# Longer runs for one weight matrix, and two array columns in place of four for another, in a decode step bound by its loads

## The chip, the cores and the metric

One core of a Trainium2 chip runs the program. The metric is device time in microseconds (us). A profile of one execution goes with each kernel; its span counts from the first to the last instruction and is some 2.3 us shorter than the time of the same execution. In its lines PE is the matmul engine (TensorE) and PEld its weight loads, DVE is VectorE, ACT ScalarE, POOL GpSimd, and SPq is the queue from which SyncE issues the loads. What is said of single DMA packets is read from the packet records in the traces, which none of the views shown here prints. One execution of the kernel before took 426.16 us. It is slow in the sense used here (over 1.5% above the fastest).

## The reference, cut to what matters

```python
x = A_x                                   # [1, 1, 1024]
xn = layernorm(x)
# A: one query token, 32 heads in 4 groups of 8, 65536 cached keys per group, head size 128
q = xn @ wq                               # [1024, 4096]
p = softmax(q k^T / sqrt(128)); o = p v   # 4 x 8 heads
A = o.reshape(1, 1, 4096) @ wo            # wo: [4096, 1024]
# B: a small MLP on the same row
x1 = xn + shifted(gelu(layernorm(xn) @ w1)) @ w2
B = x1 + gelu(layernorm(x1) @ w3) @ w4    # w3: [1024, 3584], w4: [3584, 1024]
out = x + A + B
```

With a sequence of one token the shifts leave only zeros. What is large is what has to be read: eight loads of 8.4 MB of keys, eight of values, and 35.7 MB of weights.

## The kernel before

Everything large passes through three slots of 64 KB per partition in one fixed order. A load is issued when the slot that it takes is free.

```python
stream = ["wq", "w3", "w12"]
for u in range(NU):                       # NU = 8
    if u == NU - 1:
        stream += [("K", u), "wo", ("V", u)]
    else:
        stream += [("K", u), ("V", u)]
stream.append("w4")
# ... (cut) in the loader: wo as 4 runs of 16 KB per partition, one per group
elif it == "wo":
    go(out=t[:].rearrange("p (g n) -> p g n", g=HKV),
       in_=A_wo.rearrange("(g p j) n -> p g (j n)", g=HKV, p=P))
```

The input row of w3 is replicated over a strip of 32 columns of the array (called one array column below), and four such array columns work side by side. Each reads every 28th column of w3, so that the hidden vector comes out in the order in which w4 is laid out.

```python
def row_matmul(acc, rep, cols, widths, groups=4):
    for c in range(DC):
        for i, n in enumerate(widths):
            for q in range(groups):
                nc.tensor.matmul(acc[32 * q:32 * q + 32, i, 0:n], lhsT=rep[:, c, :], rhs=cols(c, i, q),
                                 start=(c == 0), stop=(c == DC - 1),
                                 tile_position=(0, 32 * q), skip_group_check=True)

def compute_w3():
    wt = st.tiles["w3"][:, 0:DC * F].rearrange("p (c m k) -> p c k m", c=DC, k=FC)   # FC = 28
    psh = ps_S.tile([P, SUBS, 512], F32, name="psh", tag="sc")
    row_matmul(psh, xn2_rep, lambda c, i, a: wt[:, c, 16 * i:min(16 * (i + 1), FC), 32 * a:32 * (a + 1)],
               (512, 32 * FC - 512))
    st.done("w3")                         # frees the slot: V0 may be issued
    # ... (cut) two GELUs, a transpose, two copies into hT
```

The projection of the first three groups takes 48 matmuls with `oT[g][:, j]` (8 heads' worth of one group, laid out as wo's rows ask for) while V7 is still arriving; the last group's 16 come at the end.

## Time and profile before

| | kernel before |
|---|---|
| time | 400.77 us, median of 3 (400.53 to 426.16) |
| span of the profiled execution | 398.4 us |
| bytes loaded | 169.87 MB |
| time of the DMA packets, share of 16 engines' span | 99.0% |
| busiest engine | PE, 59% |

When the second and third slot were refilled for the first time, from the timeline of the DMA queue's issuer (start, length, what):

```profile
51.34 0.33 SPq L225 DMA_DIRECT2D big<-in_A_v_cache_dram  x1
58.04 0.33 SPq L225 DMA_DIRECT2D big<-in_A_k_cache_dram  x1
```

and what w3's matmuls cost, from the page's groups (operation, count, busy us, mean ns, idle before):

```profile
L330 PE MATMUL psh<-big,ln_rep_b 128*32 128x512 bf16 (+1 forms) x64 | 12.5, 947 | 3.0 <-DMA big<-in_B_w_dram 3.0
```

V0 is issued the moment the last of these is done (38.81 + 12.49 = 51.30 us).

### The profile page before, as it was taken

To read this page: it belongs to the slowest core of one execution; us is meant where nothing else is said; L and a number is where in the kernel's file an instruction comes from. 1 tells how busy PE (TensorE), PEld (TensorE's weight loads), DVE (VectorE), ACT (ScalarE), POOL (GpSimd) and SP (SyncE) were. 2 spreads that over 40 slices of the span, in tenths; PEclk is the share of its full clock that TensorE was granted. 3 is DMA by queue.
4 is the path that set the end of the run, shared out by engine and by line. 5 is a ranking of instruction groups with operands and counts; after the bars stand their busy time and mean duration, and the time that the engine had idled before them with its cause. 6 is when DMAs were issued, how large, how long until landed. Compare 5 with 4: busy or idle time off the path is not lost.

```text
span 398.4 us, 2623 instructions
## 1 busy us (share of the span) xinstructions
PE 234.3 (59%) x1372; PEld 45.1 (11%) x862; DVE 211.4 (53%) x162; ACT 27.9 (7%) x36; POOL 10.1 (3%) x38
## 2 busy tenths in 40 slices
PE   0283970591469238833974196529652956394986
PEld 0200010010100010011001010100020102000133
DVE  0602010974196569543963795259429942894132
ACT  1002010003000200020002000200010001002000
POOL 2200000000000000000000000000000000002000
PEclk9997996598869785956796889567955895698899
DMA  9998999999999999999999999999999998999996
GB/s 421 421 449 375 441 447 474 441 421 421 416 422 434 421 474 449 421 428 421 421 429 434 454 454 428 416 428 421 434 442 428 461 434 387 413 457 429 407 428 267
DMA packets 4310, 170.03 MB, mean 427 GB/s; under 512 B 457, under 2 KB 459, under 8 KB 844
## 3 DMA queue, kind: packets, MB, share of 16 engines
q1 hardware_dynamic: 4294, 169.87, 99.0%
q8 instruction: 9, 0.15, 0.1%
q14 instruction: 1, 0.01, 0.0%
q10 hardware_dynamic: 6, 0.00, 0.0%
HBM read 169.87 MB, written 0.00 MB: 426 GB/s over the span
## 4 chain that ended last, share of the span: by engine, by line
DMA 54%; DVE 21%; PE 18%; ACT 2%; another core or an unknown queue 2%; SPq 1%; POOLq 1%; issue 1%; DVEq 0%; ACTq 0%
DMA big<-in_A_k_cache_dram 41%; DVE big L410 15%; PE sc L415 11%; DMA big<-in_B_w_dram 8%; DMA big<-in_A_wq_dram 5%; PE oacc L465 4%; PE psq L330 2%; DVE p_sb L436 2%; DVE mx L420 2%; ACT p_sb L433 2%; SPq L217 1%; POOLq L613 1%; ACT L433 0%; DVE m L424 0%
## 5 line engine op out<-in xcount | busy, mean ns | idle before, releaser
L415 PE MATMUL sc<-big,qdiag 128*128 128x512 bf16 x512 | 130.7, 417 | 63.8 <-DVE big L410 63.8
L410 DVE STREAM_TRANSPOSE big<-big 128x4096 f32<-128x4096 f32 x32 | 139.4, 4412 | 47.9 <-DMA big<-in_A_k_cache_dram 47.8
L465 PE MATMUL oacc<-big,p_sb 128*32 128x512 bf16 x512 | 44.7, 518 | 34.5 <-DVE p_sb L436 34.5
L420 DVE TENSOR_REDUCE mx<-sc 128x1 f32<-128x2048 f32 x8 | 18.3, 2292 | 30.5 <-PE sc L415 30.5
L415 PEld LDWEIGHTS <-qdiag 128*128 128x128 bf16 x128 | 13.3, 104 | 176.6 <-issue 146.1
L433 ACT ACTIVATE p_sb<-sc,nball 128x2048 bf16<-128x2048 f32 x8 | 15.7, 1967 | 218.5 <-DVE nball L431 218.5
L436 DVE STREAM_TRANSPOSE p_sb<-p_sb 128x2048 bf16<-128x2048 bf16 x8 | 18.5, 2311 | 18.0 <-ACT p_sb L433 18.0
L465 PEld LDWEIGHTS <-p_sb 128*32 128x32 bf16 x512 | 16.5, 125 | 59.4 <-DVE p_sb L436 35.1
L474 DVE SCALAR_TENSOR_TENSOR og<-oacc,wb,og 128x512 f32<-128x512 f32 x4 | 3.0, 751 | 29.1 <-PE oacc L465 29.1
L508 PE MATMUL o_acc<-big,oT 128*1 128x512 bf16 x48 | 13.0, 440 | 2.4 <-ACT p_sb L433 2.4
L330 PE MATMUL psh<-big,ln_rep_b 128*32 128x512 bf16 (+1 forms) x64 | 12.5, 947 | 3.0 <-DMA big<-in_B_w_dram 3.0
L422 PE MATMUL pm_mx<-ident_f,mx 128*1 128x128 f32 x8 | 2.2, 270 | 19.1 <-DVE mx L420 19.1
L330 PE MATMUL psq<-big,ln_rep_a 128*32 128x512 bf16 x64 | 9.9, 486 | 3.9 <-DMA big<-in_A_wq_dram 3.9
L355 POOL COPY qdiag<-qx 32x32 bf16<-32x32 bf16 x16 | 3.3, 205 | 263.1 <-PE sc L415 245.4
L371 DVE STREAM_TRANSPOSE h_row<-h_row 128x896 bf16<-128x896 bf16 x1 | 1.1, 1111 | 16.2 <-ACT h_row L370 16.2
L343 DVE CAST q_row<-psq 64x1024 bf16<-64x1024 f32 x1 | 1.2, 1217 | 12.7 <-PE psq L330 12.7
L273 PE MATMUL pm_ln<-ln_rowsum_a,ones_f 128*128 128x1 f32 x2 | 0.6, 346 | 12.5 <-DVE ln_rowsum_a L271 12.5
L264 DVE STREAM_TRANSPOSE x_t<-x_row 32x256 bf16<-32x256 bf16 x4 | 2.5, 616 | 8.1 <-DMA x_row<-in_A_x_dram 8.0
L487 PE MATMUL pm_e<-ol,sel8big 128*128 128x129 f32 x6 | 1.8, 385 | 7.9 <-DVE ol L485 7.9
L259 PE MATMUL psB<-big,hT 128*32 128x512 bf16 x46 | 5.5, 380 | 0.8 <-DMA big<-in_B_w_dram 0.8
L429 PE MATMUL pm_mx<-ident_f,rep 1*128 1x1 f32 x8 | 1.8, 229 | 5.0 <-DVE rep L426 5.0
L471 ACT COPY og<-oacc 128x512 f32<-128x512 f32 x4 | 2.3, 586 | 33.9 <-PE oacc L465 25.4
(112 smaller groups left out, 77.3 us busy)
## 6 DMA issues: line engine op xcount, KB each, us to landing
big<-in_A_wo_dram SPq DMA_DIRECT2D x1, 8192.0 KB
big<-in_B_w_dram SPq DMA_DIRECT2D x1, 7168.0 KB
big<-in_B_w_dram SPq DMA_DIRECT2D x3, 2048.0 KB
big<-in_B_w_dram SPq DMA_DIRECT2D x1, 2816.0 KB
big<-in_B_w_dram SPq DMA_DIRECT2D x1, 1280.0 KB
big<-in_B_w_dram SPq DMA_DIRECT2D x1, 512.0 KB
big<-in_B_w_dram SPq DMA_DIRECT2D x1, 256.0 KB
big<-in_A_k_cache_dram SPq DMA_DIRECT2D x8
```

What stands on the lines that cost most here:

```text
L217: go(out=t[i0:i0 + 4 * k:4, WHOLE * D:(WHOLE + m) * D].rearrange("e (i n) -> e i n", i=m), in_=w4_v[m0:m0 + k * m, WHOLE, :].rearrange("(i ...
L259: return nc.tensor.matmul(psB[32 * j:32 * j + 32, :], lhsT=lhsT.to_broadcast([lhsT.shape[0], 32]), rhs=rhs, start=start, stop=False, tile_ ...
L330: nc.tensor.matmul(acc[32 * q:32 * q + 32, i, 0:n], lhsT=rep[:, c, :], rhs=cols(c, i, q), start=(c == 0), stop=(c == DC - 1), tile_positio ...
L355: nc.gpsimd.tensor_copy(out=qdiag[at, LEAD:].rearrange("p (x c) -> p x c", x=4)[:, :, 32 * a:32 * a + 8], in_=qx[at, :, 8 * g:8 * g + 8])
L410: nc.vector.transpose(out=words, in_=words)
L415: nc.tensor.matmul(sc[:, e, :], lhsT=qdiag[:, c0:c0 + P], rhs=cols[:, s, e, :, b2, :, r], start=(s == 0 and b2 == 0 and r == 0), stop=(s = ...
L420: nc.vector.reduce_max(out=mx[:], in_=sc[:].rearrange("p e n -> p (e n)"), axis=AX.X)
L433: nc.scalar.activation(out=p_sb[:], in_=sc[:], func=ACTF.Exp, bias=nball[:, b:b + 1], scale=SCALE, accum_out=group["lall"][:, b:b + 1])
L436: nc.vector.transpose(out=flat, in_=flat)
L465: mm = nc.tensor.matmul(oacc[32 * q:32 * (q + 1), :], lhsT=pT[:, e, 32 * t:32 * (t + 1)], rhs=vt[:, :, e, t, :], start=(e == 0 and t < 4), ...
L508: nc.tensor.matmul(tail["rows"][0:1, h2, :], lhsT=oT[g][:, j:j + 1], rhs=wt[:, g, j, 512 * h2:512 * (h2 + 1)], start=(g == 0 and j == 0), ...
L613: with _tile.TileContext(nc) as tc:
```

## The change

Its intent is to read wo with larger packets. The first 3072 rows, three groups of 1024, become one load in which each partition gets 24 neighbouring rows, 48 KB in one piece. Row 24p + i then lies on partition p, whereas the attention results of group g lie with row 1024g + 8p' + j on partition p'. Both agree when i = 8k + j and 3p + k = 128g + p'. So nine one-hot matmuls, one for each k and g, move the results to their new partitions. The last group is ready too late for that and keeps its layout, in a second load. Besides, w3 runs on two array columns in place of four, with four GELUs of 64 partitions in place of two of 128.

```diff
             elif it == "wo":
-                go(out=t[:].rearrange("p (g n) -> p g n", g=HKV),
-                   in_=A_wo.rearrange("(g p j) n -> p g (j n)", g=HKV, p=P))
+                go(out=t[:, 0:EARLY * D], in_=A_wo[0:EARLY * P, :].rearrange("(p i) n -> p (i n)", p=P))
+                go(out=t[:, EARLY * D:], in_=A_wo[EARLY * P:, :].rearrange("(p j) n -> p (j n)", p=P))
...
-        row_matmul(psh, xn2_rep, lambda c, i, a: wt[:, c, 16 * i:min(16 * (i + 1), FC), 32 * a:32 * (a + 1)],
-                   (512, 32 * FC - 512))
+        halves = (slice(0, 16), slice(16, FC))
+        row_matmul(psh, xn2_rep, lambda c, i, q: wt[:, c, halves[i % 2], 32 * (q + 2 * (i // 2)):32 * (q + 2 * (i // 2) + 1)],
+                   (512, 32 * FC - 512) * 2, groups=2)
...   (four GELUs in place of two: cut)
+    def regroup():
+        pick3 = ogpool.tile([P, P * (2 * HKV - 3)], BF16, name="pick3", tag="og")
+        nc.gpsimd.memset(pick3[:], 0.0)
+        nc.gpsimd.tensor_copy(out=pick3[:, P * (HKV - 2):P * (HKV - 1)], in_=ident_f[:])
+        pm = ps_M.tile([P, 512], F32, name="pm_o", tag="pm")
+        for k in range(HKV - 1):
+            for g in range(HKV - 1):
+                at = P * (HKV - 2) + k - P * g
+                nc.tensor.matmul(pm[:, 8 * k:8 * k + 8], lhsT=pick3[:, at:at + 3 * P - 2:3], rhs=oT[g][:],
+                                 start=(k == 0 and g == 0), stop=(g == HKV - 2), skip_group_check=True)
+        nc.vector.tensor_copy(out=o_early[:], in_=pm[:, 0:EARLY])
...   (project(g) split in project_early() and project_last(), same matmuls: cut)
     for u in range(NU - 1):
         compute_k(u)
+        if u == NU - 2:
+            regroup()
         compute_v(u)
```

More of the change, by code (lines that the diff above doesn't have):

```diff
@@ L155 @@
     LEAD = 8 * (SETS - 1)
+    EARLY = 8 * (HKV - 1)
     const = ctx.enter_context(tc.tile_pool(name="const", bufs=1))
@@ L316 @@
         nc.vector.tensor_copy(out=x_halves[32 * j:32 * j + 1, :], in_=x_row[0:1, 512 * j:512 * (j + 1)])
+    o_early = const.tile([P, EARLY], BF16, name="o_early")
     place = ogpool.tile([P, LEFT, P], BF16, name="place", tag="og")
@@ L364, in compute_w3 @@
         psh = ps_S.tile([P, SUBS, 512], F32, name="psh", tag="sc")
-        row_matmul(psh, xn2_rep, lambda c, i, a: wt[:, c, 16 * i:min(16 * (i + 1), FC), 32 * a:32 * (a + 1)],
-                   (512, 32 * FC - 512))
+        halves = (slice(0, 16), slice(16, FC))
+        row_matmul(psh, xn2_rep, lambda c, i, q: wt[:, c, halves[i % 2], 32 * (q + 2 * (i // 2)):32 * (q + 2 * (i // 2) + 1)],
+                   (512, 32 * FC - 512) * 2, groups=2)
         st.done("w3")
         h_row = ppool.tile([P, 32 * FC], BF16, name="h_row", tag="p")
-        nc.scalar.activation(out=h_row[:, 0:512], in_=psh[:, 0, :], func=ACTF.Gelu_apprx_tanh)
-        nc.scalar.activation(out=h_row[:, 512:], in_=psh[:, 1, 0:32 * FC - 512], func=ACTF.Gelu_apprx_tanh)
+        for i in range(4):
+            a, part = 64 * (i // 2), slice(512 * (i % 2), (512, 32 * FC)[i % 2])
+            nc.scalar.activation(out=h_row[a:a + 64, part], in_=psh[0:64, i, 0:part.stop - part.start],
+                                 func=ACTF.Gelu_apprx_tanh)
         nc.vector.transpose(out=h_row[:], in_=h_row[:])
@@ L499, in group_rows, with project_early, project_last @@
         nc.vector.tensor_scalar(out=oT[g][:], in0=o5[:], scalar1=rl[:, 0:1], scalar2=None, op0=ALU.mult)
-    def project(g):
-        wt = st.tiles["wo"][:].rearrange("p (g j n) -> p g j n", g=HKV, j=8)
+    def regroup():
[9 more added lines that the diff above has]
+        nc.vector.tensor_copy(out=o_early[:], in_=pm[:, 0:EARLY])
+    def project_early():
+        wt = st.tiles["wo"][:].rearrange("p (i n) -> p i n", n=D)
+        for i in range(EARLY):
+            for h2 in range(2):
+                nc.tensor.matmul(tail["rows"][0:1, h2, :], lhsT=o_early[:, i:i + 1], rhs=wt[:, i, 512 * h2:512 * (h2 + 1)],
+                                 start=(i == 0), stop=(i == EARLY - 1), tile_position=(0, 0))
+    def project_last():
+        wt = st.tiles["wo"][:].rearrange("p (i n) -> p i n", n=D)
         for j in range(8):
             for h2 in range(2):
-                if g == HKV - 1:
-                    mm = row_acc(h2, oT[g][:, j:j + 1], wt[:, g, j, 512 * h2:512 * (h2 + 1)])
-                    continue
-                nc.tensor.matmul(tail["rows"][0:1, h2, :], lhsT=oT[g][:, j:j + 1],
-                                 rhs=wt[:, g, j, 512 * h2:512 * (h2 + 1)], start=(g == 0 and j == 0),
-                                 stop=(g == HKV - 2 and j == 7), tile_position=(0, 0))
-        return mm.ins if g == HKV - 1 else None
+                mm = row_acc(h2, oT[HKV - 1][:, j:j + 1], wt[:, EARLY + j, 512 * h2:512 * (h2 + 1)])
+        return mm.ins
     def copy_projection():
@@ L536 @@
     tail["rows"] = ps_S.tile([P, SUBS, 512], F32, name="o_acc", tag="sc")
-    for g in range(HKV - 1):
-        project(g)
+    project_early()
     copy_projection()
@@ L551 @@
     with tc.issue_after(filled):
-        projected = project(HKV - 1)
+        projected = project_last()
     quarters = [ps_M.tile([P, 512], F32, name="pm_r", tag="pm") for _ in range(2)]
```

## The prediction

> **What bounds the kernel now.** I read, in this order: the strip of 40 slices, the table of DMA queues, the windows over single loads, what the DMA queue itself waits for, the chain at the end of the span, and last the records of the single DMA packets. From the page:
>
> ```profile
> span 398.4 us, 2623 instructions
> PE 234.3 (59%) x1372; PEld 45.1 (11%) x862; DVE 211.4 (53%) x162; ACT 27.9 (7%) x36; POOL 10.1 (3%) x38
> ...
> DMA  9998999999999999999999999999999998999996
> ...
> q1 hardware_dynamic: 4294, 169.87, 99.0%
> ```
>
> No engine is busy over 59%, but the 16 DMA engines are busy in 99.0% of the span, with no slice under 8 tenths before the last. So the kernel is a stream of 169.87 MB: wq, w3, w1 and w2, then seven K and V pairs, K7, wo, V7, w4. Its three SBUF slots are refilled early enough that the queue never runs dry. Every number of the chain of waits that reads DVE or PE is an engine waiting its turn inside that stream, not a limit. The windows below split the stream at the packets' starts: wo, V7, the two together, and a pair of plain cache loads (V6 and K7). Columns: stretch, length, busy times, clock, DMA share, GB/s.
>
> ```profile
> 337.45:357.54 20.09, 13.76 (x68) 1.76 (x25) 17.09 (x4) 0.59 (x1) 0.00 (x0) 0.81 0.99 421
> 357.54:376.38 18.84, 13.06 (x49) 2.10 (x21) 6.18 (x10) 2.24 (x3) 2.23 (x1) 0.82 1.02 443
> 337.45:376.38 38.93, 26.82 (x117) 3.86 (x46) 23.28 (x13) 2.83 (x4) 2.23 (x1) 0.81 1.01 431
> 298.75:337.45 38.70, 22.28 (x120) 4.26 (x76) 25.92 (x16) 2.06 (x2) 0.00 (x0) 0.75 1.00 434
> ```
>
> wo's own window and V7's trade time at their border (the engines are not in step, their completions lie 2 us apart), so only the pair is safe: 38.93 us with wo, 38.70 us for an equal 16.8 MB without. The short runs of wo cost **0.23 us** in all. That is the whole of what this part of the change can win.
>
> The issue side is early. In the queue's own timeline wo is issued at 324.12 and its first packet goes at 337.45:
>
> ```profile
> 324.12 0.39 SPq L205 DMA_DIRECT2D big<-in_A_wo_dram  x1
> 338.94 0.34 SPq L225 DMA_DIRECT2D big<-in_A_v_cache_dram  x1
> 363.92 2.45 SPq L217 DMA_DIRECT2D big<-in_B_w_dram  x3
> ```
>
> And the end of the span hangs on the last landing of w4 (chain of waits, last part): the last four matmuls, one addition and the store follow it within 2.0 us.
>
> ```profile
> 384.19 12.15 DMA big<-in_B_w_dram
> ...
> 396.38 0.34 PE pm_r L578 x2
> ```
>
> **What the Trainium skill says.** "DMA: Bandwidth & Descriptors", Where 436 GB/s comes from: the SBUF ports cap the traffic at 435 GB/s. The trace agrees, 434 GB/s over the pair of cache loads: nothing can be won on those. The same page, Why small descriptors are slow (HBM only), puts a fixed cost of about 3 cycles on each packet and calls grouping worth it only at 256 B or less. The trace agrees that the cost is fixed and small: packets of 16 KB took 612.5 ns in the median, of 56 KB 2116 ns, of 64 KB 2420 ns, with 4 ns between packets; per byte 16 KB is 1.2% dearer than 64 KB. "SBUF — State Buffer", Specifications, gives lines of 16 bytes and a penalty for each access that crosses to a new line. w3 is read with a step of 28 elements, 56 bytes, so each element is on a new line; its 512-column matmuls took 1052 ns, against 486 ns for wq's, which read runs of 64 bytes, so the trace fits, though wq's also differ in running on two array columns. "TensorE: Matmul & The Clock Gate", Measured speedup vs the span model, gives 2.38 times for three column tiles: four columns at once should beat two unless reading is the limit. No run here has w3 both ways.
>
> **The change part by part.**
>
> *wo in two loads.* Before, each DMA engine carries 8 partitions x 4 runs of 16 KB: 32 x (612.5 + 4) = 19.73 us. After, 8 runs of 48 KB and 8 of 16 KB. I interpolate a 48 KB packet between 16 and 56 KB: 2116 - 8192 x (1503.5 / 40960) = 1815 ns. So 8 x 1819 + 8 x 616.5 = 19.48 us: 0.25 us less, minus one more 9 ns completion. The other way: 24 packets per engine more than a cache load cost 0.23 us, and 16 of them go: 0.15 us. **Saved: 0.15 to 0.24 us**, all on the path that sets the end, because every later load moves up by it.
>
> *One more issue and one more completion counter.* 0.4 us on the queue's issuer, 13 us before the load starts: hidden. The built order shows the counters of w4's pieces shifted by one place; the waits among them remain on the same kind of load (V7 for the eighth piece, the 2 MB piece for the last), so the queue stays fed.
>
> *Nine one-hot matmuls.* They come after K6's scores and before V6, where PE waits 4.75 us for the transposed probabilities (327.6 to 332.3). 128x128 weight loads took 104 ns in the score loop; with strided one-hot weights I take up to 200 ns, and as much per tiny matmul: 9 x 0.2 to 0.4 = 2 to 3.5 us, inside the gap. The extra DVE copy of 24 columns (0.16 us, as for the similar 128x1 copy) stands in DVE's wait for K7; the memset and cast on POOL (under 1 us, from 2.23 us for w4's memset of eight times the bytes) are far earlier than needed. Even 1 us of slip would only move V7's issue from 338.94 to 340, needed by about 356: hidden.
>
> *Projection.* 48 matmuls on the first three groups before and after, 16 on the last; same shapes, same place: 0.
>
> *w3 on two columns.* 64 matmuls remain. Now they take 12.49 us (38.81 to 51.30). If reading limits all columns together, it stays near 12.5 us; if each column has its own limit, two columns take twice, 25 us. The four GELUs on 64 partitions cost 2 x (0.60 + 0.48) = 2.16 us in place of 1.08. Both delay only V0's issue (51.34) and K1's (58.04). V0's first packet is due at 66.5; a load's first packet comes 1.0 us after issue (first load), so there are 14 us of slack. 12.5 us of delay still fits, 1.5 us short of the edge. K1 has over 25 us. Time on the path: **0**.
>
> Sum: 400.77 - 0.2, about 400.5 us.
>
> **The rivals.**
>
> (a) *The whole saving is real but drowned.* The three runs of before hold two at 400.53 and 400.77: their difference equals the effect. This is what I expect.
>
> (b) *w3 doubles and starves the queue.* For: four strided columns deliver 3584 columns per 1.54 us, some 0.58 per ns and column, which looks like a limit of each column. Against: the 14 us of slack. If it overran, the gap would be 0 to 2 us once, in the slices near 66 us, and the time up to 402.5 us.
>
> (c) *Long runs change how the engines stagger.* Eight 16 KB instruction fetches inside the stream each delay one DMA engine by 1.0 to 1.5 us, on different engines, so completions of the late loads spread over 2.07 us against 0.51 us at first, and the slowest sets each landing. If the added instructions make two fetches hit one engine, the end moves by up to 1.5 us; for the better, likewise. It is not tied to the idea of the change.
>
> (d) *16 KB runs cost more in memory than their packets show.* Then wo's gain would be over 1 us. Against: the pair of windows holds the entire cost, 0.23 us.
>
> **Range and chances.** The centre is 400.5. (a) gives -0.25 to 0; (b) and (c) have perhaps one chance in six together of +0.5 to +2; runs of one kernel differ by 0.1 to 0.3%, up to 1.2 us either way. So 399.7 to 401.5. Two per cent is 8 us, more than any rival yields: 0.97 for within 2%, and the rest for slow executions (one of before's three took 426.16) or what I didn't see.
>
> **What will show it right or wrong.** The DMA share stays at 99%, with 256 packets fewer on the queue and 16 completions more, some 4054. wo with V7 takes 38.7 to 38.8 us in place of 38.93. V0 is issued between 51 and 65 us and the first loads' stretch has no gap. The nine matmuls lie in PE's gap before V6. The last landing is near 396.1 in place of 396.38. I am wrong if the time moves by over 1 us; if a zero shows in the strip near 66 us; if PE, not the DMA, ends the wait before the last matmuls; or if wo's stretch shrinks by over 0.5 us.

## The result, and the profile after

The changed kernel took **400.65 us** (median of 6, 400.43 to 400.88), the kernel before 400.78 us (median of 6). The ratio is 0.9998 with a 95% interval of 0.9984 to 1.0012. A ratio here is the mean time of one kernel's fast runs over the mean of the other's in the same rounds (a round runs each kernel of a group in turn), so it is not quite the ratio of the medians. The time alone cannot show an effect of 0.15 us, so the profile has to.

The page of the changed kernel (span; busy us, share and instructions of each engine; DMA share in 40 slices; the data queue's packets, MB and share):

```profile
span 398.3 us, 2631 instructions
## 1 busy us (share of the span) xinstructions
PE 247.7 (62%) x1381; PEld 46.0 (12%) x855; DVE 211.2 (53%) x163; ACT 28.9 (7%) x38; POOL 11.0 (3%) x40
...
DMA  9998999999999999999999999999999999999996
...
q1 hardware_dynamic: 4054, 169.87, 99.0%
```

There are 240 packets fewer on the queue (256 data packets fewer, 16 completions more), as worked out beforehand, and the share is unchanged at 99.0%. PE gained 13.4 us of busy time and the span did not notice.

The stretch of wo and V7, and the pair of plain cache loads ahead of it, in the changed kernel (stretch, length, busy times, clock, DMA share, GB/s). A stretch is cut where the last packet of a load starts: this one from K7's last packet to V7's.

```profile
337.43:376.22 38.79, 26.42 (x113) 3.71 (x42) 23.28 (x13) 2.83 (x4) 2.23 (x1) 0.82 1.01 435
298.74:337.43 38.69, 22.68 (x129) 4.72 (x85) 25.75 (x17) 2.06 (x2) 0.00 (x0) 0.74 1.00 432
```

With wo the stretch takes 38.79 us where it took 38.93: **0.14 us** won. The control beside it did not move (38.69 against 38.70). Each figure is from one profiled execution, but five of them agree: 38.93 in both kernels with the old wo, 38.78 to 38.79 in the three with the new one (the others are wo_alone, w3_alone and w3_unstrided_wrong below). The gain goes through to the end. The last data packet ends at 395.70 us against 395.85, and the chain of waits ends as before, a little earlier:

```profile
384.03 12.13 DMA big<-in_B_w_dram
396.15 0.04 issue
396.19 0.34 PE pm_r L598 x2
```

396.19 against 396.38 us for the last matmuls. So the bound is the same and the win is as small as the prediction's lower route to it.

On the other side of the ledger, w3 in the changed kernel, and what waits for it in the issuer's timeline:

```profile
L332 PE MATMUL psh<-big,ln_rep_b 128*32 128x512 bf16 (+1 forms) x64 | 24.6, 942 | 3.1 <-DMA big<-in_B_w_dram 3.1
```

```profile
63.44 0.33 SPq L226 DMA_DIRECT2D big<-in_A_v_cache_dram  x1
72.25 0.33 SPq L226 DMA_DIRECT2D big<-in_A_k_cache_dram  x1
```

w3 takes **twice as long**, V0 is issued 12.1 us later and K1 14.2 us later. K0's last packets end between 66.96 and 67.42 us on 15 of the 16 DMA engines (the sixteenth at 68.87), and V0's first packets follow each within 3 ns. The whole delay is inside the slack. The slack left is small, though: a load's first packet comes 1.0 us after its issue, so V0 could have been issued until about 66.0 us, 2.5 us later than it was.

The nine matmuls of the regrouping, and the copy of their result:

```profile
326.26 0.27 PE L427 MATMUL pm_mx<-ident_f,mx 128*1 128x128 f32 x1 [2.38 <-DVE mx L425]
326.37 0.38 PE L514 MATMUL pm_o<-oT,pick 128*128 128x8 bf16 x9
326.56 0.28 DVE L429 TENSOR_REDUCE m<-pm_mx 1x8 f32<-1x128 f32 x1 [0.36 <-PE pm_mx L427]
326.78 0.18 DVE L516 CAST o_early<-pm_o 128x24 bf16<-128x24 f32 x1
```

They take 0.38 us together, between two small transposes where PE waited for DVE anyway, and cost the path nothing.

### The profile page after: what moved, and what is told of

Same layout as the page of the kernel before. It is cut to its first block, busy times and chain, and to the rows that moved or that the text cites. A ratio compares the mean times of both kernels' runs of the same rounds, so it can differ in the third digit from the quotient of the medians.

```text
span 398.3 us, 2631 instructions
## 1 busy us (share of the span) xinstructions
PE 247.7 (62%) x1381; PEld 46.0 (12%) x855; DVE 211.2 (53%) x163; ACT 28.9 (7%) x38; POOL 11.0 (3%) x40
## 4 chain that ended last, share of the span: by engine, by line
DMA 58%; PE 20%; DVE 18%; ACT 2%; SPq 1%; POOLq 1%; issue 0%; DVEq 0%; ACTq 0%
DMA big<-in_A_k_cache_dram 41%; DMA big<-in_B_w_dram 17%; DVE big L415 14%; PE sc L420 7%; PE psh L332 6%; PE oacc L470 4%; DVE p_sb L441 2%; DVE mx L425 2%; ACT p_sb L438 2%; PE ps L392 1%; SPq L218 1%; POOLq L633 1%; ACT h_row L374 0%; PE psB L260 0%; DVE m L429 0%
## 5 line engine op out<-in xcount | busy, mean ns | idle before, releaser
L415 DVE STREAM_TRANSPOSE big<-big 128x4096 f32<-128x4096 f32 x32 | 139.4, 4412 | 30.7 <-DMA big<-in_A_k_cache_dram 30.7
L470 PE MATMUL oacc<-big,p_sb 128*32 128x512 bf16 x512 | 45.5, 526 | 34.5 <-DVE p_sb L441 34.5
L332 PE MATMUL psh<-big,ln_rep_b 128*32 128x512 bf16 (+1 forms) x64 | 24.6, 942 | 3.1 <-DMA big<-in_B_w_dram 3.1
L522 PE MATMUL o_acc<-big,o_early 128*1 128x512 bf16 x48 | 12.9, 437 | 2.4 <-ACT p_sb L438 2.4
L392 PE MATMUL ps<-big,ln_rep_b 128*32 128x512 bf16 x16 | 5.0, 485 | 2.0 <-ACT h_row L374 2.0
## 6 DMA issues: line engine op xcount, KB each, us to landing
big<-in_B_w_dram SPq DMA_DIRECT2D x1, 256.0 KB, 12.1
```

Source lines behind the costliest of these rows:

```text
L392: nc.tensor.matmul(ps1[0:32, q, :], lhsT=xn2_rep[:, c, :], rhs=wt[:, 0, c, 512 * q:512 * (q + 1)], start=(c == 0), stop=(c == DC - 1), til ...
L415: nc.vector.transpose(out=words, in_=words)
L470: mm = nc.tensor.matmul(oacc[32 * q:32 * (q + 1), :], lhsT=pT[:, e, 32 * t:32 * (t + 1)], rhs=vt[:, :, e, t, :], start=(e == 0 and t < 4), ...
L522: nc.tensor.matmul(tail["rows"][0:1, h2, :], lhsT=o_early[:, i:i + 1], rhs=wt[:, i, 512 * h2:512 * (h2 + 1)], start=(i == 0), stop=(i == E ...
```

## The experiments

**Theory.** The DMA engines never pause, so the time is bytes plus a fixed cost per packet. The whole effect of the change is 16 packets less on each engine. w3's doubling is real and lies in the slack of one load's issue. **Rivals:** the slower w3 costs something that hides a larger gain; 16 KB runs cost more than their packets show; or there is a threshold of run length rather than a cost per packet; and on w3, the number of columns or the weights, not the step between elements, sets its pace.

Runs of one group were timed on the same chip together with the kernel before: the first four (before: 400.8 us, median of 11), the next three (400.88 us, median of 9), and the last (400.85 us, median of 9).

One caution on correctness. Four of these kernels put rows or columns in wrong places, and the comparison with the reference passed them nevertheless. So it does not resolve what wo and w3 contribute here, and that it passes the changed kernel says little about the regrouping. For that there is only the index equation above, which I checked against the slice of the one-hot tile by hand: column 256 + p' of that tile is one on row p', and the slice takes column 256 + k - 128g + 3p.

### wo_alone: the loads and the regrouping without w3's change

```diff
 # changed kernel, with compute_w3() of the kernel before (four columns, two GELUs)
```

> The loads of wo and the regrouping as in the changed kernel, w3 on four columns as before. Theory (wo's packets are the only thing on the path): the whole effect of the change is here: wo with V7 takes 38.79 us as in the changed kernel against 38.93 before, the last packet ends 0.15 us earlier than before, V0 is issued near 51.3, the time lies 0.1 to 0.2 us under before, too little for the rounds to tell. Rival (the slower w3 costs something that hides part of the gain): this one is over 0.3 us faster than the kernel before.

Measured: 400.47 us (median of 5, 400.21 to 401.51), ratio 0.9999 (0.9987 to 1.0011). The stretch of wo and V7, cut in the same way at its own packets:

```profile
337.58:376.37 38.79, 26.38 (x113) 3.70 (x42) 23.28 (x13) 2.83 (x4) 2.23 (x1) 0.82 1.01 435
```

38.79 us, as in the changed kernel; the last data packet ends at 395.72 us. The rival, a larger gain hidden by w3, is out: without w3's change there is no more to be had.

### w3_alone: two columns, wo as before

```diff
 # kernel before, with compute_w3() of the changed kernel (two columns, four GELUs)
```

> w3 on two columns and four GELUs, wo as before. Theory (each strided column has its own limit, and the delay is inside the slack): w3's matmuls take 24 to 25 us, V0 is issued near 63.4 in place of 51.3, the DMA share has no hole near 66 us, wo with V7 takes 38.93 us, the time equals before within 0.2 us. Rival (the later issue leaves a hole at V0): over 0.5 us slower than before, and V0's first packet later than 66.5.

Measured: 400.78 us (median of 5, 400.39 to 401.74), ratio 1.0006 (0.9994 to 1.0018). w3's matmuls take 24.6 us, V0 is issued at 63.43 us. The stretch of wo and V7:

```profile
337.33:376.26 38.93, 25.61 (x96) 3.36 (x34) 23.28 (x13) 2.83 (x4) 2.23 (x1) 0.82 1.01 433
```

38.93 us, as before, and the last data packet ends at 395.94 us (before: 395.85, so that this end scatters by 0.1 us where the stretch does not). So w3's 12 us of extra work cost nothing that these rounds or the profile can see, and the 0.14 us belong to wo alone.

### wo_64k_wrong, wo_4k_wrong, wo_2k_wrong: the length of a run as a dose

All three are the kernel before with one line changed. All instructions stay, only the packets differ. Their outputs are wrong, which doesn't matter for the times. The shorter the runs, the longer the issuer was held when it issued V7 behind wo: 0.33 us with runs of 64 KB, 9.03 with 4 KB, 15.31 with 2 KB (337.52 to 352.83 us). V7's first packets still followed wo's without a gap, at 359.36 us and later, so this cost nothing here.

```diff
-                go(out=t[:].rearrange("p (g n) -> p g n", g=HKV),
-                   in_=A_wo.rearrange("(g p j) n -> p g (j n)", g=HKV, p=P))
+                go(out=t[:], in_=A_wo.rearrange("(p i) n -> p (i n)", p=P))           # 64 KB
+                go(out=t[:].rearrange("p (i n) -> p i n", i=16),                      # 4 KB; i=32: 2 KB
+                   in_=A_wo.rearrange("(i p r) n -> p i (r n)", i=16, p=P))
```

> Kernel before with the whole of wo as one run of 64 KB per partition, the rows in the wrong places on purpose; all instructions the same. It is the most that longer runs could give. Theory: wo with V7 takes 38.70 us as a pair of cache loads does, 0.23 us under before; the time 400.5 us, not to be told from before. Rival (16 KB runs cost more than their packets show): 1 us or more faster.

> Kernel before with wo as 16 runs of 4 KB per partition, rows in the wrong places on purpose; all instructions the same. Theory (fixed cost per packet): 128 packets per engine of 159 + 4 ns are 20.9 us in place of 19.7, the kernel 1.1 to 1.2 us or 0.3% slower than before, between before and the 2 KB runs. Rival (a threshold at some run length): equal to before, or equal to the 2 KB runs.

> Kernel before with wo read as 32 runs of 2 KB per partition; the rows land elsewhere, so the result is wrong on purpose; all instructions are the same. Theory (a packet's cost is 8 to 9 ns of its own plus 4 ns between, nothing else): 256 packets per engine of 84 + 4 ns are 22.5 us in place of 19.7, so wo with V7 takes 41.7 us and the kernel 403.5 us, 2.8 us or 0.7% over before. Rival (short runs cost more in memory than packets of that size in w4 showed): over 4 us slower. Rival (it is hidden, as other waits bound the end): under 1 us slower.

The stretch of wo and V7 of the three, in this order:

```profile
337.48:376.18 38.70, 25.66 (x98) 3.41 (x33) 23.28 (x13) 2.83 (x4) 2.23 (x1) 0.82 1.00 434
```

```profile
337.44:377.27 39.83, 26.84 (x103) 3.56 (x35) 23.28 (x13) 2.83 (x4) 2.23 (x1) 0.83 1.02 422
```

```profile
337.40:378.44 41.04, 28.18 (x113) 3.95 (x40) 23.28 (x13) 2.83 (x4) 2.23 (x1) 0.79 1.03 409
```

| wo in runs of | packets per engine | wo and V7, us | last data packet ends, us | ratio to before (95%) |
|---|---|---|---|---|
| 64 KB | 8 | 38.70 | 395.62 | 0.9994 (0.9981 to 1.0006) |
| 48 and 16 KB (changed kernel) | 16 | 38.79 | 395.70 | 0.9998 (0.9984 to 1.0012) |
| 16 KB (before) | 32 | 38.93 | 395.85 | 1 |
| 4 KB | 128 | 39.83 | 396.78 | 1.0029 (1.0011 to 1.0047) |
| 2 KB | 256 | 41.04 | 398.15 | 1.0058 (1.0045 to 1.0070) |

The medians were 400.50 us (5 runs), 401.56 (4 runs, 401.44 to 401.58 and one of 403.16) and 402.86 (6 runs). The column of the stretch is a straight line. From 8 to 256 packets it grows by 2.34 us over 248 packets, 9.4 ns each; from 8 to 128 by 1.13 us over 120, 9.4 ns each; from 8 to 32 by 0.23 us over 24, 9.6 ns each. There is no threshold, and no cost of short runs beyond the packet. The end follows: the last packet moves by 2.30 us between 16 KB and 2 KB, and the ratio of 1.0058 is 2.3 us (in part by luck: the four runs without the side effect below lie 2.0 us over before, the other two 3.2 and 3.4). Both forecasts were too high, 2.8 us for 2 KB and 1.1 to 1.2 us for 4 KB, where the stretches grew by 2.11 and 0.90 us, because I had added 4 ns of gap to each packet's own time. This gap had the wrong sign: in the records the next packet starts 3 to 4 ns before the last one ends. In the 2 KB run a packet of wo lasts 88 ns and the next one starts after 84.4. And even wo in single runs of 64 KB, for which this kernel has the last group's results too late, is at 400.5 us. The idea has no more than 0.23 us in it.

A side effect of the 2 KB runs: two of the six executions took 403.90 and 404.14 us, the other four 402.53 to 402.91. The profiled one is one of the two. Its last 22 matmuls before the final sums took 3.87 us at a granted clock of 0.64, where the kernel before took 2.55 us at 1.00; the matmuls had been waiting for their data for 1.55 us, 0.46 us before. So in this execution the extra microsecond is the array's clock and not the loads. What lowered the clock was not tested, and the other slow execution has no profile.

```profile
393.70:397.60 3.90, 3.87 (x22) 1.48 (x21) 0.00 (x0) 0.00 (x0) 0.00 (x0) 0.64 0.86 350
```

### w3_unstrided_wrong: the same matmuls, neighbouring columns

```diff
-        wt = st.tiles["w3"][:, 0:DC * F].rearrange("p (c m k) -> p c k m", c=DC, k=FC)
+        wt = st.tiles["w3"][:, 0:DC * F].rearrange("p (c f) -> p c f", c=DC)
...
-        ... wt[:, c, halves[i % 2], 32 * (q + 2 * (i // 2)):32 * (q + 2 * (i // 2) + 1)],
+        ... wt[:, c, 896 * (q + 2 * (i // 2)) + halves[i % 2].start * 32:896 * (q + 2 * (i // 2)) + halves[i % 2].stop * 32],
```

> Changed kernel with w3's matmuls reading runs of 512 and 384 neighbouring columns in place of every 28th, on the same two array columns; the hidden vector comes in another order, so the result is wrong on purpose. Theory (the step of 56 bytes is what limits each column): the 64 matmuls take 8 to 10 us, as wq's 64 on two columns take 9.8, in place of 24.6. Rival (two columns or the weights limit it): 20 us or more. The time stays within 0.3 us of before either way.

Measured: one look, 400.75 us. The group of w3's matmuls:

```profile
L332 PE MATMUL psh<-big,ln_rep_b 128*32 128x512 bf16 (+1 forms) x64 | 8.7, 449 | 3.4 <-DMA big<-in_B_w_dram 3.4
```

8.7 us in place of 24.6, with the same 64 matmuls on the same two columns. The step of 56 bytes costs a factor of 2.8. The array's clock is not the cause: it was lower in the faster run (0.71 over these matmuls, against 0.88 in the changed kernel). Together with the equal means of 947 ns on four columns and 942 ns on two this gives the mechanism: with this step each array column goes at its own slow pace, whatever the others do, so half the columns take twice the time. V0 was issued at 47.64 us, 16 us earlier than in the changed kernel, and the time is the same.

### w3_late and w3_late_half: where the slack ends

```diff
+        for n_extra in range(2):          # 1 in w3_late_half: the first 8 matmuls once more each, results discarded
+            for i in range(4):
+                for q in range(2):
+                    nc.tensor.matmul(psh[32 * q:32 * q + 32, i, 0:(512, 32 * FC - 512)[i % 2]], lhsT=xn2_rep[:, 0, :], ...)
         row_matmul(psh, xn2_rep, lambda c, i, q: ...)
```

> Changed kernel with the first 8 matmuls of w3 done three times (16 more matmuls, results discarded, result right). Theory (the slack of V0's issue ends at 65.5 us, and beyond it every us of delay is lost for good): w3 takes 24.6 + 6.1 us, V0 is issued at 69.6, its first packet comes at 70.6 in place of 66.4, the engines stand still 4.1 us, the time is 404.7 us, about 4 us or 1.0% over the changed kernel. Rival (the stream runs ahead of its users and makes the hole good later): under 1 us slower.

Measured: 405.79 us (4 runs, 405.75 to 405.88), ratio 1.0127 (1.0114 to 1.0140), span 403.5 us. The issuer's timeline and the DMA share in 40 slices of that run:

```profile
70.55 0.33 SPq L226 DMA_DIRECT2D big<-in_A_v_cache_dram  x1
76.84 0.33 SPq L226 DMA_DIRECT2D big<-in_A_k_cache_dram  x1
```

```profile
DMA  9998994999999999999999999999999999999996
```

The 4 in the seventh slice (60.5 to 70.6 us) is the hole; the changed kernel has a 9 there. Nothing later makes it good: the last data packet ends 5.17 us later than in the changed kernel, and the time is 5.1 us longer. So the rival falls, and the slack is a real edge. My 4.1 us was too small. V0 was issued 0.95 us later than I had worked out, as the matmuls took 31.7 us in all and not 30.7, and the engines' first packets after the stop took 2906 to 3434 ns in place of 2420. The account from the packets: the engines stood still 4.37 us in the mean, and their first packet took 0.72 us longer in the mean. That is 5.09 us.

> Changed kernel with the first 8 matmuls of w3 done twice (8 more, results discarded, result right): half the dose of the run w3_late, at the edge of the slack. From w3_late: a matmul costs 0.40 us more, so V0 is issued at 63.4 + 3.2 to 3.6 = 66.6 to 67.0, its first packet follows 1.0 us later at 67.6 to 68.0, and 15 of 16 engines, whose K0 packets end between 66.4 and 66.9, stand still some 1.0 to 1.4 us. Theory A (a stop costs the gap and, besides, 0.5 to 1.0 us as first packets after a stop are slower): the time is 1.6 to 2.2 us over the changed kernel. Theory B (a stop costs the gap alone): 1.0 to 1.4 us over. Rival (small holes are made good later): under 0.5 us over.

Measured: 402.0 us (median of 5, 401.55 to 402.33), ratio 1.0023 (1.0009 to 1.0037). V0 was issued at 66.46 us, half a microsecond beyond the edge:

```profile
66.46 0.33 SPq L226 DMA_DIRECT2D big<-in_A_v_cache_dram  x1
```

V0's first packets started at 67.42 us and later, so the engines stood still only 0.60 us in the mean, not 1.0 to 1.4: I had taken K0 to end on most engines at 66.4 to 66.9 us, half a microsecond too early. Their first packets took 0.61 us longer in the mean (up to 3700 ns). Gap and slow start together are 1.21 us, the gap alone 0.60. The ratio says 0.9 us with an interval from 0.4 to 1.5, the medians 1.15. Both theories' ranges as I had written them were off with the gap, and the time alone doesn't decide between them, nor quite exclude the rival's 0.5 us; that the first packets after the stop are slower stands in the packets' records of both runs. In the profiled execution, the slowest of the five (402.33 us), the last data packet ended 1.84 us later than in the changed kernel. That is more than the mean engine's 1.21; the engine that was already last (K0 until 68.78 us) stood still for 0.80 us and then took 3700 ns for its first packet, 2.08 us in all. So there a small hole was not made good either.

## Why the prediction was right, point by point

- **The bound.** Right. The strip and the 99.0% are unchanged, and the chain still ends on w4's landing.
- **wo's packets, 0.15 to 0.24 us.** Right at the lower route: 0.14 us in the stretch, 0.15 us at the last packet, in the changed kernel (0.14 and 0.13 in wo_alone). The upper route was mis-sized by its gap term, "with 4 ns between packets". The records of neighbouring packets overlap by 3 to 4 ns instead, so the term had to be subtracted, and the same sum then gives 0.11 us. The runs give 9.4 ns per packet in all, so 16 packets are 0.15 us. The interpolated 48 KB packet was 1815 ns and came out at 1819 ns. One reading was wrong without harm: at 337.45 us goes not wo's first packet but the last one of K7, wo's first goes at 337.82; as all its windows are cut in this way, their lengths hold.
- **The extra issue and the shifted counters.** Right. The two loads were issued at 323.91 and 324.28 us, V7 and w4 as early as before.
- **The nine matmuls, 2 to 3.5 us.** The cost on the path was right, at zero, but the size was five to nine times too large: 0.38 us for the nine. I had added up weight loads and matmuls one after the other. They overlap: the matmuls start every 26 ns, though each is recorded at 167 ns and each weight load at 103. The place was wrong too: they ran at 326.37 us, not in the gap of 4.75 us before V6 but in the short one between the two transposes, and the copy stood between two DVE steps there, not in the wait for K7. Neither moved what follows: the second transpose starts 0.89 us after the first, as before.
- **w3, 12.5 or 25 us.** The second of the two came true, 24.6 us; the prediction left that open. w3_unstrided_wrong shows why. That its cost on the path is zero was right, and its slack, put at 14 us with V0's first packet due at 66.5, was 14.6, as that packet was due at 66.92; 12.1 were used. w3_late and w3_late_half show that this slack was the thing that mattered and where it ends. The four GELUs took 1.93 us, where 2.16 had been expected.
- **Rival (c), instruction fetches.** The changed kernel has nine fetches like the kernel before, and their effects were of the same size (completions 1.94 us apart at V7, 2.06 before). It did not come into play; no run tests it.
- **The time.** 400.5 predicted, 400.65 measured, within the range. The effect of 0.15 us is seen in the records of the packets, and not in the time, where two executions differ by more. That is rival (a). Rival (d), costs of 16 KB runs beyond their packets, fell with wo_64k_wrong.

## What to carry to other kernels

When the load queue is 99% busy, cut its stream at packet starts, compare a stretch with an equal one without the suspected cost, and the difference is the most that a rearrangement of that load can win; here that sum took one line and gave 0.23 us before anything was built. Off the bound, look not at how much an engine's work grows but at the latest moment at which the next load may be issued: 12 us of extra matmuls were free, 2.5 more would have been, and beyond that the time grew by at least what was overrun. Check, too, whether the comparison with the reference sees the part that you changed at all.

## What the Trainium skill lacked or had wrong

- "DMA: Bandwidth & Descriptors", Why small descriptors are slow (HBM only), gives a fixed cost in cycles and advises grouping only at 256 B or less. It has no measured time per packet for large runs. Here it is 9.4 ns per packet and engine, the same from 2 KB to 64 KB; a load of 8.4 MB in runs of 2 KB takes 2.3 us (12%) longer than in runs of 64 KB.
- The same page gives latencies of a single DMA but nothing on what a stop of a busy queue costs besides its own length: the first packet of 64 KB on each engine after a stop took 3138 ns in the mean (w3_late) and 3028 ns (w3_late_half) against 2420 ns.
- "SBUF — State Buffer", Specifications, states a penalty for each access to a new 16-byte line without its size. For a bf16 moving operand with a step of 56 bytes it was a factor of 2.8 (24.6 against 8.7 us for the same 64 matmuls).
- "TensorE: Matmul & The Clock Gate", Measured speedup vs the span model, does not say what packing columns does when the moving operand is strided. Here four columns took 12.5 us and two took 24.6 us at equal means per matmul (947 and 942 ns): the columns do not share the penalty.
- "Runtime: NRT & Kernel Launch", Instruction fetch mechanics, says that instructions are fetched in blocks of 16 KiB and that the cost of crossing into the next block is mostly hidden. The traces agree on the blocks (nine packets of 16 KB). It doesn't say that the fetch takes time from the loads: each took about 1.05 us on one DMA engine and prolonged the data packet that followed it there by about 0.5 us. From the first fetch on, the engines' completions of one load lay 2 us apart (0.51 us before it).
